# Top-k attention into a mixture of experts on one core: some scores computed ahead and kept in DRAM

## The chip, the core and the metric

One core of a Trainium2 chip runs the whole program. The metric is device time in microseconds (us) of one execution. TensorE (PE) multiplies, VectorE (DVE) searches, ScalarE (ACT) copies and exponentiates, GpSimd (POOL) subtracts and scatters, SyncE (SP) issues most DMAs.

## What is computed

Attention of 8 batches and 8 heads over 576 positions with head size 64, where each row keeps only its 32 largest scores; its output, 4608 rows of 512, goes row by row to the one of 8 experts with the largest gate logit (512 to 1024, ReLU, 1024 to 512).

```python
scores = scale * np.matmul(q, k.transpose(0, 1, 3, 2))
kth = np.partition(scores, -top_k, axis=-1)[..., -top_k:-top_k + 1]
scores = np.where(scores >= kth, scores, -1e9)
attn = softmax(scores)                        # over the last axis
x = np.matmul(attn, v)                        # then (B, S, H*D) -> (4608, 512)
expert_idx = np.argmax(x @ w_gate, axis=1)
# per expert e, for its rows:
y = np.maximum(x_e @ w1[e], 0.0) @ w2[e]
out = gate_w[:, None] * y
```

All of it is float32.

## The kernel before

**Work items.** Two heads make a unit, four units a batch (counted from 0 here and in the code). A row tile is 128 queries of one head; a work item is two row tiles, one of each head of a unit, or the four 64-row tails of two units. So a pair of units has nine items and a batch 18: unit 0's four, a tail item, unit 1's four, and the same again. `loop` (L906) runs over the 144 items in order; one turn is called a slot. Its order is written out by hand for PE, ACT and DVE (`manual_schedule`, L987); SP's and GpSimd's order is left to the scheduler.

**One slot i.** DVE folds the scores of item i+1 (`fold`, L290 and L292; `fold_on`, L298 and L300, late in the slot) and searches the 32nd largest of item i (L329 to L345). ACT turns the threshold into an offset (`low`, L354; `depths`, L370), GpSimd subtracts (`less`, L379), ACT exponentiates (`weights`, L387), PE transposes the weights of item i-1 (`transposed`, L398 to L411) and ACT copies them out (L404, L402, L419). At the end of the slot PE computes the scores of item i+4 (`multiply`, `products`, L276) into two PSUM tiles, which ACT copies into one of four `s` buffers (`scores`, L283) in the next slot. So scores are made with AHEAD = 3 slots in hand. `multiply` also loads the q and k of the unit after next (L141).

**A unit's end.** `ending` is a generator that advances at named places of the slot: attention times v (`outputs`, L432, copied by ACT to oT, L434), its transposition with the gate logits (L443, L450), the divisors (`divisors`: ACT L454 and L455, DVE's reciprocal L457 as one of the small steps in `aside`, of which `tick` puts one behind each search instruction), then GpSimd's `logits` (L465 to L470) and `rows` (L478). After the fourth unit come the choice of the expert, the rank of each row within its expert (`ranks`), and the scatter of the rows to `x_rows` in DRAM (L545).

**Expert blocks.** 128 rows of one expert are a block. `ahead` loads rows and weights of the next blocks on SP (L634, L636, L642; 2 MB each for w1 and w2, two buffers each). `turned` transposes the block's rows (L662, copied by ACT at L664 as xTs); `block` then yields 16 pieces: eight of the first product (L687, four matmuls each) and eight of the second (L702). `pieces(n)` runs up to n of them and stops a block that pauses. Where `current` is None it takes the next loaded block if that was loaded at least ON_CHIP = 3 slots ago. `following`, called within a block, stores results and turns the next block's rows. Each slot deals `now` pieces from a credit: a rate by batch, times a share by the tile, 0.5 to 1.6 (L946). New blocks of a batch reach the list in slot 13 of the next one; a number fixed when the program is built is dealt per batch, and the last 14 blocks and some held back run after the attention, on PE alone.

**PSUM.** `ps_s` has two score tiles; `ps_t` two banks that wTm, wTl, po and px take in turn.

The changed loop's callers are the main body from L734; the code below L1004 runs only where rows stay in doubt.

Of the kernel before, what the change touches and what calls it, by code (L numbers as in the profile page):

```python
# [9 lines left out]
F32 = mybir.dt.float32  # L10
# [25 lines left out]
def kernel(  # L36
# [6 lines left out]
    moe_w2: bass.AP,  # L43
    out: bass.AP,
):

# [34 lines left out]
    nc = tc.nc  # L83
    B, U, P, _ = qk.shape
    N, Dm = out.shape
# [644 lines left out]
    ON_CHIP = 3  # L730
    KEEP = 3 * PIECES
    BETWEEN = 2

    with fast:  # L734
        units = [(b, u) for b in range(B) for u in range(U)]
# [12 lines left out]
        def landed(n):  # L748
            return clock is None or clock - n.at >= ON_CHIP
# [16 lines left out]

        def following():
            put_stores()
            if loaded and landed(loaded[0]):
                turned(loaded[0])  # L770

        def pieces(n):
            nonlocal current, left
            while n > 0 and left > 0:
                if current is None:
                    if not landed(loaded[0]):
                        break
                    current = block(loaded.pop(0), following, stores.append)
                    ahead()
                if clock is None:  # L780
                    evacuate()
                step = next(current)
                if step == "pause":
                    if clock is not None:
                        break
                    continue
                if step == "last":
                    current = None
                n -= 1
                left -= 1  # L790
            return n
# [11 lines left out]
        def ending(b, u):  # L803

            nonlocal left
            n = unit[b * U + u]
            if u == 0:
                x_of[b] = k.xp.tile([P, KC, XW], F32, name="x")
                in_turn(token_ids(x_of[b][:, :, Dm + 1].bitcast(I32), b))
                lg_of[b] = k.small.tile([P, KC, E], F32, name="lg")  # L810
            x, lg = x_of[b], lg_of[b]
            out_steps = outputs(n, x)
            yield "products"
            next(out_steps)
            yield "relu"
            next(out_steps)
            if u % 2 == 0:
                yield "relu"
            div = divisors(n)
            next(div)  # L820
            aside.append(div)
            yield "products"
            next(out_steps)
            if b * U + u + 2 < len(units):
                load_values(unit[b * U + u + 2])
            yield "relu"
            next(out_steps)
            yield "products"
            next(out_steps)
            yield "relu"  # L830
            next(out_steps, None)
            yield "rows"
            through(div)
            logits(n, lg)
            rows(n, x)
            if u < U - 1:
                return
            yield "small"
            r = choice(lg)
            aside.append(r.steps)  # L840
            yield "weights"
            yield "turn"
            through(r.steps)
            nc.scalar.activation(lg, lg, AF.Exp)
            yield "products"
            ranks(r)
            yield "small"
            steps = places(r, x)
            aside.append(steps)
            yield "relu"  # L850
            nc.scalar.copy(run, r.run)
            yield "pool"
            through(steps)
            scatters.extend(scattering(r, x))
            if b == B - 1:
                scatter(KC)
                slot_i = k.small.tile([1, 2, NSLOT], I32, name="slot_i")
                through(table(slot_i, SURE, False))
                firsts = [(slot_i[0:1, 0, j:j + 1], slot_i[0:1, 1, j:j + 1]) for j in range(SURE)]
                ready = load_rows(SimpleNamespace(), firsts[0][1], True)  # L860
            new = LAST - SURE if b == B - 1 else new_of[b]
            if new:
                slot_i = slot_last if b == B - 1 else k.small.tile([1, 2, NSLOT], I32, name="slot_i")
                steps = table(slot_i, new, b == B - 1)
                aside.append(steps)
                yield "weights"
                yield "pool"
                yield "weights"
                yield "pool"
                through(steps)  # L870
                coming.extend((slot_i[0:1, 0, j:j + 1], slot_i[0:1, 1, j:j + 1]) for j in range(new))
            if b == B - 1:
                spare.extend(coming[ALWAYS - SURE:])
                del coming[ALWAYS - SURE:]
                assert len(loaded) == 2 and not waiting
                fill_up()
                coming[0:0] = [(firsts[0][0], ready)] + [(expert, (piece,)) for expert, piece in firsts[1:]]
                scatter(0)
# [9 lines left out]

        got_of, s_of, f_of, w_of = {}, {}, {}, {}

        def tiles_of(i):
            b, g = work[i]
            return [(unit[b * U + u], tile) for u, tile in g]
# [3 lines left out]

        def multiply(i):
            tiles = tiles_of(i)
            got_of[i] = products(tiles)  # L900
            n, tile = tiles[0]
            more = n.b * U + n.u + 2
            if tile == (NC - 1 if n.u % 2 else 2 * NC) and more < len(units):
                unit.append(load_unit(*units[more]))

        def loop():  # L906
            nonlocal credit, rate, clock
            for i in range(min(AHEAD, len(work))):
                multiply(i)
                s_of[i], steps = scores(got_of.pop(i))  # L910
                for step in steps:
                    step()
            multiply(AHEAD)
            f_of[0] = fold(s_of[0])
            fold_on(f_of[0])
            for i, (b, g) in enumerate(work):
                tiles = tiles_of(i)
                u, tile = g[0]
                if tile == 0 and u % 2 == 0:
                    open_unit(tiles[0][0])  # L920
                if tails(tiles):
                    open_unit(tiles[1][0])

                then = lambda: None
                if i + 1 < len(work):
                    f_of[i + 1] = fold(s_of[i + 1])
                    then = lambda: fold_on(f_of[i + 1])
                low, nbias, doubts = search(tiles, s_of[i], f_of.pop(i), then)
                at_place("small")
                w_of[i] = depths(s_of[i], low)  # L930
                less(s_of.pop(i), w_of[i])
                doubts()
                put_stores()
                scatter(1)
                at_place("pool")
                at_place("relu")
                at_place("rows")
                at = i % per_batch
                if at == FIRST and b:
                    rate = new_of[b - 1] * PIECES / (U * NT)  # L940
                credit += rate * len(g)
                room = left
                if b == B - 1 and at >= ARRIVED:
                    room -= KEEP
                    credit = room / (len(work) - i)
                share = {0: 0.5, 1: 1.2, 2: 1.6, 3: 0.5, 2 * NC: 1.4}[tile]  # L946
                now = max(0, min(int(credit * share + 0.5), room))
                credit -= now
                clock = i
                if i + AHEAD < len(work):  # L950
                    s_of[i + AHEAD], steps = scores(got_of.pop(i + AHEAD))
                    for step in steps:
                        step()
                evacuate()
                at_place("turn")
                turns = turning(i - 1) if i else iter(())
                next(turns, None)
                part = min(BETWEEN, now - now // 2)
                rest = pieces(part)
                next(turns, None)  # L960
                rest = pieces(now - now // 2 - part + rest)
                weights(tiles, w_of[i], nbias)
                next(turns, None)
                evacuate()
                if i + AHEAD + 1 < len(work):
                    multiply(i + AHEAD + 1)
                if tile == NC - 1:
                    end = ending(b, u)
                    late.append([end, next(end)])
                at_place("products")  # L970
                at_place("weights")
                credit = min(credit + pieces(now // 2 + rest), 6 * rate)
# [147 lines left out]
```

## Time and profile before

| what | us |
| --- | --- |
| median of ten runs (1371.31 to 1374.38) | 1373.01 |
| the profiled execution | 1372.41 |
| its span | 1370.8 |
| PE busy | 1232.0 (90%) |
| DVE busy | 1084.9 (79%) |
| ACT busy | 931.9 (68%) |
| POOL busy | 661.7 (48%) |
| granted TensorE clock, mean | 0.949 |

A line of the profile's groups reads: line, engine, operation, output from inputs, shape, number of instructions, then total busy time and mean of one in ns, then the idle time in front and what ended it. Timelines give start and length in us. A matmul of float32 appears as two instructions, and their lengths overlap, so the pace of PE is read from starts, not from lengths. DMA rows give size and median time from issue to landing.

### The profile page before, as it was taken

How to read it: one execution, taken by the hardware profiler on the slowest of the kernel's cores; microseconds unless marked ns; L12 is line 12 of the kernel's file. 1: busy time of each engine (PE TensorE's matmuls, PEld its weight loads, DVE VectorE, ACT ScalarE, POOL GpSimd, SP SyncE). 2: the span in 40 equal slices, each digit the busy share in tenths (PEclk: the TensorE clock that was granted, in tenths of full speed). 3: DMA queues.
4: the chain of work that ended last, by engine and by line, in shares of the span. 5: the costliest groups of instructions: out<-in, count | busy, mean ns of one | idle time of the engine just before them, and what ended most of it. 6: DMA issues, size and time to landing. Idle time of an engine off the chain costs nothing. (4 is left out here: it accounts for less than half of the span.)

```text
span 1370.8 us, 24487 instructions
## 1 busy us (share of the span) xinstructions
PE 1232.0 (90%) x7666; PEld 836.5 (61%) x7666; DVE 1084.9 (79%) x4591; ACT 931.9 (68%) x2113; POOL 661.7 (48%) x805
## 2 busy tenths in 40 slices
PE   5777677677799999999999999999999999999995
PEld 3444444344466666766666666767676677776773
DVE  8999999999999999999999999999999820000000
ACT  4788878877888888888877788887777821111110
POOL 3455556555654666566556665565557621000000
PEclk9888887887899999999999999999999999999998
DMA  2000011001573267427654474357542859989880
GB/s 82 29 29 29 28 36 56 29 29 44 182 291 121 92 235 263 141 73 257 231 173 168 162 277 149 113 187 293 184 167 80 303 183 367 383 323 330 302 317 19
DMA packets 102220, 231.68 MB, mean 169 GB/s; under 512 B 5182, under 2 KB 25918, under 8 KB 102080
## 3 DMA queue, kind: packets, MB, share of 16 engines
q1 hardware_dynamic: 95328, 209.76, 43.1%
q0 software_dynamic: 6464, 19.97, 4.0%
q8 instruction: 62, 1.02, 0.3%
q14 instruction: 78, 0.64, 0.1%
q10 hardware_dynamic: 288, 0.30, 0.1%
HBM read 208.72 MB, written 22.33 MB: 169 GB/s over the span
## 5 line engine op out<-in xcount | busy, mean ns | idle before, releaser
L379 POOL TENSOR_TENSOR w<-s,w 128x576 f32<-128x576 f32 x288 | 410.1, 1445 | 432.6 <-ACT w L370 432.6
L687 PE MATMUL ph<-xTs,w 128*128 128x128 f32 x2560 | 308.5, 276 | 6.0 <-ACT xTs L664 6.0
L687 PEld LDWEIGHTS ph<-xTs,w 128*128 128x128 f32 x2560 | 297.5, 192 | 26.2 <-issue 18.9
L702 PE MATMUL py<-w,hT 128*128 128x512 f32 x640 | 292.2, 596 | 0.0
L338 DVE MAX8 tops<-scr 128x8 f32<-128x168 f32 x864 | 245.4, 315 | 0.0
L276 PE MATMUL sc<-qkb 64*128 64x288 f32 (+1 forms) x1280 | 220.6, 470 | 9.5 <-ACT s L283 5.2
L387 ACT ACTIVATE w<-w,nbias 128x576 f32<-128x576 f32 x288 | 224.1, 792 | 2.9 <-POOL w L379 2.0
L370 ACT ACTIVATE w<-s,low 128x576 f32<-128x576 f32 x288 | 207.6, 768 | 4.7
L398 PE MATMUL wTm<-turn,w 128*128 128x128 f32 x1152 | 170.4, 288 | 29.0 <-ACT xl L450 18.9
L999 DVE CAST any_i<-pd 1x1 int32<-1x1 f32 x1 | 0.1, 146 | 236.0 <-PE pd L997 236.0
L398 PEld LDWEIGHTS wTm<-turn,w 128*128 128x128 f32 x1152 | 132.1, 145 | 89.2 <-issue 34.9
L702 PEld LDWEIGHTS py<-w,hT 128*128 128x128 f32 x640 | 114.4, 190 | 117.6 <-issue 116.5
L345 DVE MATCH_REPLACE8 scr<-tops,scr 128x168 f32<-128x168 f32 x576 | 176.9, 311 | 0.0
L283 ACT COPY s<-sc 128x576 f32<-128x576 f32 x288 | 169.1, 641 | 11.0 <-PE sc L276 11.0
L404 ACT COPY wT<-wTm 128x512 f32<-128x512 f32 x256 | 139.1, 604 | 38.9 <-PE wTm L398 38.6
L276 PEld LDWEIGHTS sc<-qkb 64*128 64x128 f32 (+1 forms) x1280 | 117.9, 195 | 72.5 <-issue 26.1
L432 PE MATMUL po<-wT,vb 128*64 128x288 f32 x1024 | 158.6, 459 | 0.4 <-ACT wTt L419 0.4
L708 POOL DMA_INDIRECT out_dram<-y,xg x40 | 43.2, 1079 | 211.7 <-ACT y L716 199.6
L329 DVE MAX8 few<-l 128x8 f32<-128x288 f32 x288 | 127.2, 442 | 0.0
L432 PEld LDWEIGHTS po<-wT,vb 128*64 128x64 f32 x1024 | 75.8, 153 | 79.0 <-issue 31.7
L290 DVE TENSOR_TENSOR h<-s 128x576 f32<-128x576 f32 x144 | 118.4, 822 | 5.8 <-ACT s L283 5.8
L692 ACT ACTIVATE hT<-ph 128x512 f32<-128x512 f32 x80 | 48.6, 608 | 107.3 <-PE ph L687 107.2
(116 smaller groups left out, 1428.8 us busy)
## 6 DMA issues: line engine op xcount, KB each, us to landing
w<-in_moe_w_dram SPq DMA_DIRECT2D x80, 2048.0 KB, 9.6
qkb<-in_qk_dram SPq DMA_DIRECT2D x31, 608.0 KB, 4.0
xg<-x_rows SPq DMA_DIRECT2D x40, 257.0 KB, 9.8
vb<-in_v_dram SPq DMA_DIRECT2D x32, 320.0 KB, 3.2
x_rows<-blank SPq DMA_DIRECT2D x5, 257.0 KB, 13.9
x_rows<-blank POOLq DMA_DIRECT2D x4, 257.0 KB, 8.6
x_rows<-x,posi POOLq DMA_INDIRECT x40, 3.1
out_dram<-y,xg POOLq DMA_INDIRECT x40, 6.1
```

The costliest lines, as they stand in the source:

```text
L276: nc.tensor.matmul(ps[rows, j, 0:HF], n.q[d, cols], n.k[d, keys], start=True, stop=True)
L283: lambda m=m, ps=ps: nc.scalar.copy(s[:, m, :, :], ps[:, :, 0:HF]) for m, ps in enumerate(got)
L338: nc.vector.max(out=tops[:, m, r * 8:(r + 1) * 8], in_=src[m])
L345: nc.vector.match_replace(out=scr[:, m, :], in_to_replace=tops[:, m, r * 8:(r + 1) * 8], in_values=src[m], imm_value=NEG,)
L370: nc.scalar.activation(w[:, m, :], s[:, m, :, :].rearrange("p j k -> p (j k)"), AF.Relu, scale=-STEEP, bias=low[:, m:m + 1],)
L379: k.last_pool = in_turn(nc.gpsimd.tensor_tensor(w[:, m, :], s[:, m, :, :].rearrange("p j k -> p (j k)"), w[:, m, :], op=ALU.subtract)).ins
L387: nc.scalar.activation(w[:, m, :], w[:, m, :], AF.Exp, scale=scale, bias=nbias[:, m:m + 1], accum_out=n.z[:, c:c + 1])
L398: nc.tensor.transpose(pm[:, c * P:(c + 1) * P], w[:, m, first:first + P], ident)
L404: nc.scalar.copy(wT[:, :, m, q], pm4)
L432: nc.tensor.matmul(po[r, 0:HF], n.v[:, c, r], rhs, start=(c == 0), stop=(c == KC - 1))
L687: nc.tensor.matmul(ph[:, f, :], n.w1[:, 0, dt, fc * P:(fc + 1) * P], n.xT[:, dt, :], start=(dt == 0), stop=(dt == DT - 1),)
L702: nc.tensor.matmul(py, hT[:, f, :], n.w2[:, 0, f, :], start=(f == 0), stop=(f == FT - 1))
```

## The change

Four edits.

1. `EARLY_FOR = (4, 5, 6)`. For the four full items of unit 1 in each of these batches (items 5 to 8 of 18), a DRAM tile of 128 x 1152 numbers (576 KB) is set up. A generator `earlier` computes their scores: in each second slot of the first 48 (i odd), between the first transposes and the first pieces, it makes two products of one head into a `sc` tile and copies it on ACT; every second step stores both heads to DRAM on SP. The q and k of a unit (608 KB) sit meanwhile in buffers of the pool `wp`, which otherwise holds w1 and w2. `multiply` leaves these items' products out, and `fetch_scores` loads the stored scores into the `s` buffer on SP in place of ACT's copies.
2. In batches 4 to 6 the share is raised by 0.35 in the slots whose `multiply` has nothing to do, and lowered by 0.1 in the others.
3. A block starts in `pieces` only where its rows have been turned already. `following` turns them if that hasn't been done, and is also called once a slot, behind the weights, where no block is under way.
4. In `ending` the divisors' reciprocal is appended to `aside` one place later, behind the next "relu".

```diff
+    EARLY_FOR = (4, 5, 6)
...
         def following():
             put_stores()
-            if loaded and landed(loaded[0]):
+            if loaded and landed(loaded[0]) and not hasattr(loaded[0], "xT"):
                 turned(loaded[0])
...
                 if current is None:
-                    if not landed(loaded[0]):
+                    if clock is not None and not hasattr(loaded[0], "xT"):
                         break
...
             div = divisors(n)
             next(div)
-            aside.append(div)
             yield "products"
             next(out_steps)
             if b * U + u + 2 < len(units):
                 load_values(unit[b * U + u + 2])
             yield "relu"
             next(out_steps)
+            aside.append(div)
             yield "products"
...
+        early = {}
+        for i, (b, g) in enumerate(work):
+            if b in EARLY_FOR and g[0][0] == 1 and g[0][1] < NC:
+                early[i] = dram.tile([P, 2, 2, HF], F32, name=f"early{i}")
+
+        def earlier():
+            todo = sorted(early)
+            own = []
+            def open_own(p):
+                if p * NC >= len(todo):
+                    return
+                room = k.wp.tile([P, 1, DT, F], F32, name="w1") if p % 2 == 0 else k.wp.tile(
+                    [P, 1, FT, Dm], F32, name="w2")
+                room = room.rearrange("p a b c -> p (a b c)")
+                nc.sync.dma_start(room[:, 0:2 * S + ST], qk[work[todo[p * NC]][0], 1, :, :])
+                own.append(room)
+            open_own(0)
+            for at, i in enumerate(todo):
+                if at % NC == 0:
+                    open_own(at // NC + 1)
+                room = own[at // NC]
+                first = 2 * S + ST + (at % 2) * 2 * S
+                put = room[:, first:first + 2 * S].rearrange("p (m j k) -> p m j k", m=2, j=2)
+                cols = slice((at % NC) * P, (at % NC + 1) * P)
+                for m in range(2):
+                    ps = k.ps_s.tile([P, 2, SM], F32, name="sc")
+                    d = slice(m * D, (m + 1) * D)
+                    for j in range(2):
+                        keys = slice(S + (0 if m else ST) + j * HF, S + (0 if m else ST) + (j + 1) * HF)
+                        nc.tensor.matmul(ps[:, j, 0:HF], room[d, cols], room[d, keys], start=True, stop=True)
+                    nc.scalar.copy(put[:, m, :, :], ps[:, :, 0:HF])
+                    if m:
+                        nc.sync.dma_start(early[i], put)
+                    yield
...
-            got_of[i] = products(tiles)
+            got_of[i] = None if i in early else products(tiles)
...
+        def fetch_scores(i):
+            got = got_of.pop(i)
+            if got is None:
+                s_of[i] = k.att.tile([P, 2, 2, HF], F32, name="s", bufs=4)
+                nc.sync.dma_start(s_of[i], early[i])
+                return
+            s_of[i], steps = scores(got)
+            for step in steps:
+                step()
...
                 share = {0: 0.5, 1: 1.2, 2: 1.6, 3: 0.5, 2 * NC: 1.4}[tile]
+                if b in EARLY_FOR:
+                    share += 0.35 if i + AHEAD + 1 in early else -0.1
...
                 next(turns, None)
+                if i % 2:
+                    next(ahead_of, None)
                 part = min(BETWEEN, now - now // 2)
...
                 weights(tiles, w_of[i], nbias)
                 next(turns, None)
+                if current is None:
+                    following()
                 evacuate()
```

More of the change, by code (lines that the diff above doesn't have):

```diff
@@ L904, in multiply @@
                 unit.append(load_unit(*units[more]))
+        def fetch_scores(i):
[7 more added lines that the diff above has]
+                step()
         def loop():
             nonlocal credit, rate, clock
+            ahead_of = earlier()
             for i in range(min(AHEAD, len(work))):
                 multiply(i)
-                s_of[i], steps = scores(got_of.pop(i))
-                for step in steps:
-                    step()
+                fetch_scores(i)
             multiply(AHEAD)
@@ L950, in loop @@
                 if i + AHEAD < len(work):
-                    s_of[i + AHEAD], steps = scores(got_of.pop(i + AHEAD))
-                    for step in steps:
-                        step()
+                    fetch_scores(i + AHEAD)
                 evacuate()
```

## The prediction

> **What bounds the kernel now.** Batches are counted from 0, as in the code, so the change speaks of batches 4 to 6; a slot is one work item, 18 to a batch. I read the 40 slices first, then a table of windows cut at the batches (by the starts of the fold L290), then the timelines of single slots.
>
> ```profile
> PE   5777677677799999999999999999999999999995
> DVE  8999999999999999999999999999999820000000
> PEclk9888887887899999999999999999999999999998
> ```
>
> Through the attention VectorE shows no idle; from slice 11 TensorE shows none either, and it goes on alone for the last seven slices. Which of the two sets the pace is told by the batches (columns: window, length, busy time of PE, PEld, DVE, ACT, POOL, granted clock):
>
> ```profile
> core 0: us, PE busy (x) PEld busy (x) DVE busy (x) ACT busy (x) POOL busy (x), PEclk, DMA share, GB/s
> 138.50:268.00 129.50, 95.83 (x538) 56.94 (x538) 129.50 (x558) 105.09 (x244) 74.24 (x93) 0.83 0.12 39
> 268.00:398.30 130.30, 101.47 (x602) 64.16 (x603) 130.30 (x573) 104.94 (x243) 73.27 (x92) 0.83 0.35 125
> ...
> 532.40:668.00 135.60, 131.91 (x873) 90.22 (x871) 134.38 (x572) 113.84 (x260) 82.98 (x98) 1.00 0.50 177
> 668.00:813.40 145.40, 144.17 (x963) 100.78 (x962) 142.02 (x573) 115.54 (x265) 87.14 (x99) 1.00 0.56 198
> 813.40:949.00 135.60, 131.90 (x872) 90.23 (x871) 134.38 (x573) 113.82 (x260) 82.98 (x98) 1.00 0.50 178
> ```
>
> The same 573 VectorE instructions take 130.3 us in batch 2, where TensorE is idle for 28.8 us, and 135.6, 145.4, 135.6 us in batches 4, 5, 6, where it is idle for 3.7, 1.2, 3.7. So 130.3 us is VectorE's floor, and the 5.3, 15.1 and 5.3 us above it come from TensorE. In batch 1 TensorE has 33.7 us to spare and ScalarE 24.4. Batch 7 and the tail are TensorE's again, so what TensorE gains in batches 4 to 6 reaches the end unless it is given back as new idle.
>
> **The change, part by part.**
>
> *Products taken out of batches 4 to 6.* Twelve items (four of each batch) lose their score products and two ScalarE copies. One item's products, L276, run from their own start to that of the next group:
>
> ```profile
> 663.38 1.24 PE L276 MATMUL sc<-qkb 64*128 64x288 f32 x8
> 664.55 0.64 PE L443 MATMUL px<-turn,oT 128*128 128x144 f32 x3
> ```
>
> That is 1.17 us, so 4.7 a batch and 14.0 in all. The copies, 24 of 641 ns, are 15.4 us of ScalarE, which is not the bound; I count nothing for them.
>
> *Pieces dealt anew.* By the built order of instructions batches 4, 5 and 6 hold 68, 76 and 68 block pieces before and after; none leaves for the tail. The largest lump grows: slot 1 of batch 5 gets 13 pieces (before 9), slot 2 none (before 4). Over both the sum is equal: 0 us.
>
> *What is given back.* TensorE can't run ahead of what the slot's search releases:
>
> ```profile
> 610.00 0.66 PE L398 MATMUL wTm<-turn,w 128*128 128x128 f32 x4
> 611.70 0.66 PE L398 MATMUL wTm<-turn,w 128*128 128x128 f32 x4 [1.05 <-ACT oT L434]
> ```
>
> Here, in slot 9 of batch 4, it already waits 1.05 us for a bank that ScalarE empties only behind that slot's search. By then it is 4 x 1.17 = 4.7 us lighter, but VectorE can come forward only by its own stalls: slots 4 and 7 took 9.41 and 9.11 us between starts of L290, 7.66 and 7.89 in batch 2, so 1.75 + 1.22 = 3.0. The other 1.7 us turn into idle: 3.4 us for batches 4 and 6. Batch 5 has 15.1 us of room and keeps its 4.7. Bounds: 0 (the stalls at the batch's end shrink too), and 2 x 4.7 = 9.4.
>
> *Early scores.* 24 steps, in each second slot of the first 48, each two products of one head and a copy of 0.64 us. The trace shows no such step: at least half an item, 0.6 us of TensorE; at most four instructions of 0.40 us side by side in time, 1.6 us, and 1.9 at the clock of 0.83. I take 1.2. Cover: TensorE's 33.7 us and ScalarE's 24.4 us idle in batch 1, 1.9 and 1.4 a slot. What pays is not the sum but the lateness: each copy stands ahead of the slot's two exponentials, so ScalarE, and behind it the subtraction on GpSimd (L379), end later, and GpSimd meets VectorE's folds. What that costs is in the trace:
>
> ```profile
> 202.83 1.48 POOL L478 TENSOR_TENSOR x<-xl,rz 128x640 f32<-128x640 f32 x1
> 203.58 1.33 DVE L290 TENSOR_TENSOR h<-s 128x576 f32<-128x576 f32 x1
> ```
>
> The fold, 0.73 us elsewhere, waits until L478 ends: 0.6 us. I take such a stall in 3 or 4 of 24 steps, +2 us; bounds 0 and 24 x 0.6 = 14.4, nearer to 0 because ScalarE's spare time of two slots, 2.7 us, exceeds copy and wait (0.64 + 1.2).
>
> The Trainium skill (TensorE: Matmul & The Clock Gate, Part 3, The mechanism) speaks against this step: small products overlap when they sit in different row groups, and the step takes one head, so one row group. The trace agrees that pairs overlap, since eight instructions of 0.40 us fit into 1.24. By the rule an early item costs double, 2.3 us, or 28 in all; were early TensorE the bound, that would turn the sum to the slow side, but its rows there are idle for 33.7 us a batch.
>
> *Stores and fetches.* Three loads of 608 KB and twelve stores of 576 KB fall into slices with DMA at 0 to 2 tenths: nothing. They stand on SP's queue among the loads of qk and v; each of those is issued some four slots ahead of its use. The twelve fetches wait on SP until GpSimd has left a score buffer, about 5 us into slot i, and are needed at the start of slot i+2: 2 x 7.2 - 5 = 9.4 us. The nearest rows:
>
> ```profile
> w<-in_moe_w_dram SPq DMA_DIRECT2D x80, 2048.0 KB, 9.6
> qkb<-in_qk_dram SPq DMA_DIRECT2D x31, 608.0 KB, 4.0
> ```
>
> Alone a fetch has 5.4 us to spare. The built order puts six of them right behind a weights load, where qk landed after 7.9 us (579.01 to 586.89): 1.5 us to spare, less wherever ScalarE lags. Queued behind them on SP are weights that are needed a block later. I take +1 us; bounds 0 (and a gain of the DVE waits for L283, 5.8 us in all) and 6 x 1.0 = 6.
>
> *First blocks' rows ahead.* Five batches (3 to 7) under TensorE's bound begin their first block with a wait:
>
> ```profile
> PE ph L687 <- ACT xTs L664: 6.0, 6, 1.1
> ```
>
> Now the rows are turned behind wTl (L411), then come 1.17 us of products, then the block. But the copy L664 moves behind both exponentials (2 x 0.79 + 2 x 0.21 = 2.0 us) and wTt's 0.27: with y's copy (0.58) and its own 0.5 xTs is ready 3.3 us behind wT's copies, and TensorE gets there in 0.16 + 0.44 + 1.17 = 1.8. Wait 1.5 instead of 1.2: +0.3 each, +1.5. Bounds: -6.0 (all gone) and +2.8.
>
> *Reciprocals.* Queued for VectorE a slot later. DVE rz waited 2.5 us each in batches 5 and 7, where TensorE sets the pace: 0, at best -2.5.
>
> **Sum**: -14.0 + 3.4 + 2 + 1 + 1.5 = -6.1. The profiled execution took 1372.4 us (span 1370.8, 1.6 around it), the median of the ten is 1373.0; from the first 1366.3, from the median 1366.9.
>
> **Rivals.**
> *More arrives*: the xTs waits vanish (-6.0 in place of +1.5): 1366.9 - 7.5 = 1359.4. For it: 1.17 us of cover is the wait's own size. Against: the copy's new place.
> *Nothing arrives*: the fetches are late and VectorE becomes the bound of batches 4 and 6. Three fetches there that stand 3.1 us too long behind weights, within the 3.9 us that these cost qk (7.9 against 4.0), eat the two batches' 9.4 us: 1373.0 - 14.0 + 9.4 + 2 + 1 + 1.5 = 1372.9. For: a margin of 1.5 us, and at SP one waiting weights load holds all behind it (L634 waited 75.8 us for L687). Against: TensorE's backlog takes up a short VectorE stall.
> *Slower*: the early steps. All 24 make GpSimd collide with a fold: 1373.0 - 14.0 + 3.4 + 14.4 + 1 + 1.5 = 1379.3; it decides from 8.1 / 24 = 0.34 us a step. VectorE has no idle there, so every stall counts in full. Against: ScalarE's 1.4 us spare a slot.
> That the change does nothing is out: the built order shows the twelve items' products gone, 48 early ones added.
>
> **How the numbers follow.** A measurement here tells 0.2% (2.7 us) from no change. Forecast 1361 to 1370: 0.52, all faster. More arrives: 0.10. Nothing arrives: 0.17, of which 0.14 within 0.2% and 0.03 slower. Slower: 0.21, of which 0.02 within. Faster 0.62, same 0.16, slower 0.22. The range, 1359 to 1376, holds the forecast, half of the better case, nearly all of the third and 0.07 of the slow one.
>
> **What will show it.** Batches 4, 5, 6 at about 132.6, 140.7, 132.6 us, with more PE waits on oT (L438 in the new lines). Batches 0 to 2 at 127.7, 129.5, 130.3 us plus at most 2 in all; more there is the slow rival. DVE waits on the DMA s<-early would be late fetches, PE waits on xTs above 1.2 us the moved rows. I am wrong if batches 4 and 6 don't shorten though early slots cost nothing: then TensorE was not their bound.

## The result and the profile after

The changed kernel takes 1378.95 us (median of eight, 1375.88 to 1379.51) against 1372.96 for the kernel before, timed beside it: ratio 1.0040, 95% interval 1.0031 to 1.0048. It is slower by 5.5 us where 6.1 us less was forecast. Its profiled execution took 1378.43 us, span 1376.8, 6.0 more than before. A second set of runs of the same kernel gave 1378.38 us, ratio 1.0037 (1.0022 to 1.0051).

The slices of the changed kernel's page answer to the three rows shown of before:

```profile
PE   6888888787899999999999999999999999999995
DVE  8999999999999999999999999999999820000000
PEclk9797889887899999999999999999999999999998
```

TensorE is a little busier in ten of the first eleven slices, VectorE as full as before. The windows, cut at the changed kernel's own batches (1, 2, 4, 5, 6; columns as before):

```profile
core 0: us, PE busy (x) PEld busy (x) DVE busy (x) ACT busy (x) POOL busy (x), PEclk, DMA share, GB/s
139.00:270.10 131.10, 107.80 (x580) 64.95 (x579) 131.10 (x558) 109.51 (x254) 77.21 (x95) 0.86 0.17 57
270.10:405.30 135.20, 114.76 (x642) 72.06 (x642) 135.20 (x572) 110.38 (x253) 74.95 (x93) 0.87 0.39 138
538.00:673.40 135.40, 128.47 (x841) 88.42 (x840) 135.40 (x573) 109.41 (x252) 83.52 (x98) 0.99 0.55 195
673.40:819.30 145.90, 142.27 (x933) 100.06 (x932) 142.08 (x571) 112.67 (x258) 84.29 (x99) 0.99 0.60 213
819.30:954.10 134.80, 127.05 (x838) 86.85 (x837) 134.80 (x573) 108.55 (x251) 83.18 (x98) 1.00 0.56 196
```

Batches 4, 5 and 6 last 135.4, 145.9 and 134.8 us (135.6, 145.3, 135.6 before), although TensorE now is idle for 6.9, 3.6 and 7.8 us of them in place of 3.7, 1.2 and 3.7. TensorE's busy time in the three fell by 10.2 us and its idle time rose by 9.7: the work was taken off it and became idle time. Batches 1 and 2 grew by 1.6 and 4.9 us, without any idle time of VectorE: the same instructions took longer.

The waits of the changed kernel over the whole program (engine, line, what ended the wait: sum, times, longest):

```profile
PE ph L691 <- ACT xTs L668: 6.5, 6, 1.3
PE wTm L402 <- ACT oT L438: 6.2, 9, 1.2
...
DVE pos L528 <- ACT run L856: 4.7, 2, 2.9
...
PE wTm L402 <- DVE pos L528: 4.1, 2, 2.0
```

Before, TensorE waited 3.5 us for oT (4 times) and not for `pos`, the rank of a row within its expert. The wait for xTs, 6.0 before, is 6.5. In batches 4 to 6 alone (window 532:955) the changed kernel has the 4.1 us for `pos` and

```profile
PE wTm L402 <- ACT oT L438: 2.3, 4, 1.1
PE wTm L402 <- ACT xl L454: 2.0, 2, 1.0
```

where the kernel before has 2.1 us for oT and none for `xl` or `pos`. So the new idle of these batches is not the wait for oT that the prediction named; that one grew with the old dealing only (`core` and `no_share`, below).

Where the six microseconds are, from the starts of the fold of each batch's first item:

| us | before | changed | difference |
| --- | --- | --- | --- |
| batches 0 to 2 | 387.4 | 394.4 | +7.0 |
| batch 3 | 134.1 | 132.7 | -1.4 |
| batches 4 to 6 | 416.6 | 416.1 | -0.5 |
| batch 7 | 130.2 | 130.4 | +0.2 |
| from there to the end of the span | 291.6 | 292.3 | +0.7 |

So two things are to be explained: why the early steps cost several microseconds, and why 14 us of TensorE's work brought half a microsecond.

### The profile page after: what moved, and what is told of

Same layout as the page of the kernel before. It is cut to its first block, busy times and chain, and to the rows that moved or that the text cites. A ratio compares the mean times of both kernels' runs of the same rounds, so it can differ in the third digit from the quotient of the medians.

```text
span 1376.8 us, 24546 instructions
## 1 busy us (share of the span) xinstructions
PE 1260.2 (92%) x7666; PEld 853.7 (62%) x7666; DVE 1094.8 (80%) x4591; ACT 931.2 (68%) x2113; POOL 661.8 (48%) x805
## 5 line engine op out<-in xcount | busy, mean ns | idle before, releaser
L383 POOL TENSOR_TENSOR w<-s,w 128x576 f32<-128x576 f32 x288 | 410.1, 1445 | 438.5 <-ACT w L374 438.4
L280 PE MATMUL sc<-qkb 64*128 64x288 f32 (+1 forms) x1184 | 216.1, 472 | 9.6 <-ACT s L287 5.2
L287 ACT COPY s<-sc 128x576 f32<-128x576 f32 x264 | 154.8, 640 | 9.9 <-PE sc L280 9.9
L408 ACT COPY wT<-wTm 128x512 f32<-128x512 f32 x256 | 138.9, 601 | 32.9 <-PE wTm L402 32.4
L294 DVE TENSOR_TENSOR h<-s 128x576 f32<-128x576 f32 x144 | 114.8, 797 | 4.0 <-ACT s L287 3.1
```

The source lines that it names most:

```text
L280: nc.tensor.matmul(ps[rows, j, 0:HF], n.q[d, cols], n.k[d, keys], start=True, stop=True)
L287: lambda m=m, ps=ps: nc.scalar.copy(s[:, m, :, :], ps[:, :, 0:HF]) for m, ps in enumerate(got)
L383: k.last_pool = in_turn(nc.gpsimd.tensor_tensor(w[:, m, :], s[:, m, :, :].rearrange("p j k -> p (j k)"), w[:, m, :], op=ALU.subtract)).ins
L408: nc.scalar.copy(wT[:, :, m, q], pm4)
```

## What an early step costs: one slot of batch 2

Slot 7 of batch 2 took 7.89 us before and 10.26 in the changed kernel. The timeline of that slot before (start, length, engine, line, operation; parts of it):

```profile
319.00 0.21 ACT L354 ACTIVATE low<-tops 128x2 f32<-128x2 f32 x1 [0.15 <-DVE tops L338]
320.10 2.84 POOL L379 TENSOR_TENSOR w<-s,w 128x576 f32<-128x576 f32 x2 [4.44 <-ACT w L370]
322.79 0.17 DVE L589 CAST ci<-run 1x8 int32<-1x8 f32 x1
323.13 0.18 DVE L591 TENSOR_SCALAR ci<-ci 1x8 int32<-1x8 int32 x1
```

And in the changed kernel:

```profile
319.44 2.28 PE L928 MATMUL sc<-w 64*128 64x288 f32 x4
...
321.76 0.64 ACT L929 COPY w<-sc 128x576 f32<-128x576 f32 x1 [1.63 <-PE sc L928]
...
324.50 0.20 ACT L358 ACTIVATE low<-tops 128x2 f32<-128x2 f32 x1
...
325.59 2.78 POOL L383 TENSOR_TENSOR w<-s,w 128x576 f32<-128x576 f32 x2 [7.00 <-ACT w L374]
325.66 1.37 DVE L593 CAST ci<-run 1x8 int32<-1x8 f32 x1
...
327.19 1.20 DVE L595 TENSOR_SCALAR ci<-ci 1x8 int32<-1x8 int32 x1
```

ScalarE waits 1.63 us for the early product and copies it, and only then come the two exponentials and `low`: 2.7 us into the slot, 0.1 before. So GpSimd's two subtractions (L383) start at 325.59, in the very moment at which VectorE handles the eight counters `ci`. A cast of eight numbers takes 1.37 us in place of 0.17 and ends when the first subtraction ends; the next takes 1.20 in place of 0.18 and ends with the second. VectorE is "busy" all that time. The same slot in seven kernels shows a dose and its effect:

| kernel | `low` starts in the slot at | the slot lasts |
| --- | --- | --- |
| before | 0.11 us | 7.89 us |
| placed (below) | 0.11 | 7.89 |
| placed_early_only (below) | 0.57 | 8.30 |
| early_only (below) | 1.73 | 9.11 |
| core (below) | 1.79 | 9.18 |
| changed, second set | 2.32 | 9.82 |
| changed | 2.74 | 10.26 |

The other seven kernels below fall into the same order: 0.12 and 0.17 us go with 7.89 and 7.88, three times 0.55 or 0.56 with 8.28 or 8.29, 1.13 with 8.94 and 2.00 with 9.52. Where the reciprocals are moved, 0.19 us of the slot is one of them.

All of batches 0 to 2 can be accounted for in this way. Take what each VectorE instruction needs above the lower quartile of its form (same operation, tiles and shape) in the kernel before, leave out differences under 0.1 us, and add up: call this the excess. It is 3.6 us before and 10.6 in the changed kernel, and the 7.0 between them are the whole growth. Each of the ten instructions that lose at least 0.5 us (two before) starts while a GpSimd instruction runs and ends no sooner than that one.

## The experiments

Each kernel was timed beside the kernel before. "Batches" are lengths in its profiled execution.

### Early steps alone (early_only)

Against the changed kernel: dealing, first rows and reciprocals as before, and the stored scores aren't used; batches 4 to 6 compute their own.

```diff
-            got_of[i] = None if i in early else products(tiles)
+            got_of[i] = products(tiles)
```

> The early products, copies and stores alone; the stored scores are not used, the 12 items keep their own products, and the dealing, the first blocks' rows and the reciprocals are as before. Theory A (the early steps stall VectorE in batches 0 to 2, and nothing came back later): batches 0 to 2 lengthen by about 7 us in all, as in the changed kernel (128.1, 131.1, 135.2 us), batches 3 to 7 stay, the time is about 1380. Theory B (the loss of batches 0 to 2 comes from the moved reciprocals or rows): batches 0 to 2 as before within 1 us, the time 1373 to 1375.

1377.08 us, ratio 1.0025 (1.0015 to 1.0035): +3.4 us. Batches 0 to 2 392.7 (+5.3), batch 3 132.3 (-1.8), batches 4 to 6 unchanged at 416.6. The early steps cost 3.4 us by themselves; the moved reciprocals and rows aren't needed for that. The loss is where the first theory put it, and smaller than its 7 us. Of the 5.3 us, 1.1 are VectorE's waits for the divisors (`rz`), which the changed kernel, with its moved reciprocals, doesn't have there.

### First blocks' rows alone (first_only)

Of the change only the turning of first rows ahead: no early scores, reciprocals as before.

```diff
-    EARLY_FOR = (4, 5, 6)
+    EARLY_FOR = ()
```

> Only the first blocks' rows turned ahead; no early scores, dealing and reciprocals as before. Theory A: between -1.5 and +1.5 us. Theory C (the copy of the turned rows, now behind both exponentials, delays ScalarE and so GpSimd and the folds): +3 us or more, with the folds L302 and L304 lengthened in slots 15 to 17.

1375.50 us, ratio 1.0010 (1.0001 to 1.0020): +1.4 us. Batch 3 grows by 0.4 and batches 4 to 6 by 0.9 together; TensorE's wait for xTs rises from 6.0 to 7.1 us. The price agrees with the 1.5 us foretold; its interval is 0.1 to 2.7.

### The change without the rows ahead (no_first)

```diff
-                if current is None:
-                    following()
```

with the two conditions on `xT` back to `landed`.

> The changed kernel with the first blocks' rows turned as before. Theory A: 1379, within 1.5 us of the changed kernel. Theory C: 1375 or less, with slots 15 to 17 of batches 4 to 6 shorter by 1 us.

1374.66 us, ratio 1.0009 (0.9999 to 1.0018). Without them the changed kernel is 4 us faster by the ratios, more than the rows cost alone. Batches 4 to 6 take 415.4 us, 0.7 less than in the changed kernel; the rest of the difference lies in batches 0 to 3, 524.0 against 527.1. That is one execution each, and such stretches scatter: the next kernel has the same instructions as the changed one there, and took 525.3. Of the 3.1 us, 2.5 lie before slot 14 of batch 2, up to where the two kernels have the same instructions in the same order on every engine, so they can't come from the rows. Nor does the sign of the theory that came nearer in time show: slots 15 to 17, which were to be 1 us shorter, are 0.3 us shorter in batches 4 and 6 and no shorter in batch 5.

### The change with pieces dealt as before (no_share)

```diff
-                if b in EARLY_FOR:
-                    share += 0.35 if i + AHEAD + 1 in early else -0.1
```

> The changed kernel with the pieces dealt as before. Theory A (TensorE's relief turns into its own idle because VectorE and GpSimd bound batches 4 and 6): 1379, batches 4 to 6 together 416 us as in the changed kernel. Theory D (the new dealing eats the gain, by the 13 pieces of slot 1 of batch 5 and by fuller late slots): batches 4 to 6 together 408 to 411 us, the time 1371 to 1374.

1373.43 us, ratio 0.9999 (0.9988 to 1.0009). Batches 4 to 6 take 411.0 us against 416.1: the dealing, put down at 0 in the prediction, costs 5.1 us there and some 5.6 by the ratios. That is what the second theory foretold (408 to 411 us, 1371 to 1374).

### The changed kernel again (after_again)

> The changed kernel once more, so that it stands beside the parts on one chip: 1.004 of the kernel before, as before, if nothing but chance lies between the calls; nearer to 1.002 if its first rounds were drawn high.

1378.38 us, ratio 1.0037. Batches 0 to 3 take 527.4 us and batches 4 to 6 415.6, close to the first profile.

### Early scores alone (core)

The first of the four edits alone: dealing, rows and reciprocals as before.

> Only the early scores: computed, stored and fetched, with dealing, first blocks' rows and reciprocals as before. Theory A (the late part keeps some 5.5 us of its 14.0 because TensorE turns the rest into waits for ScalarE's oT, for the rank bank and for a late fetch, and the early part costs 3 to 5): batches 4 to 6 together 411 us (416.5 before, 416.1 changed), batches 0 to 2 together 391 to 394, the time 0.997 to 1.000 of the kernel before. Theory D' (rows and reciprocals matter too): 1.001 or more.

1372.64 us, ratio 0.9999 (0.9986 to 1.0011): no change. Batches 0 to 3 525.3 (+3.8), batches 4 to 6 411.7 (-4.9). The idea of the change, by itself, returns what it costs. In batch 5, which was to keep 4.7 us, 0.7 is left: 145.3 to 144.6.

### Early steps in another place (placed)

Against `core`: a step takes one half of both heads, whose products run side by side, into two banks of the blocks' first product; it stands behind the slot's exponentials, so ScalarE copies it when `low` is not waiting.

```diff
-                for m in range(2):
-                    ps = k.ps_s.tile([P, 2, SM], F32, name="sc")
-                    d = slice(m * D, (m + 1) * D)
-                    for j in range(2):
+                for j in range(2):
+                    both = [k.ps_m.tile([P, SM], F32, name="ea", tag="m") for m in range(2)]
+                    for m, ps in enumerate(both):
+                        d = slice(m * D, (m + 1) * D)
...
-                if i % 2:
-                    next(ahead_of, None)
                 part = min(BETWEEN, now - now // 2)
...
                 weights(tiles, w_of[i], nbias)
                 next(turns, None)
+                if i % 2:
+                    next(ahead_of, None)
```

> As the last, but an early step makes both heads' products of one half side by side, into the block's two PSUM banks (free until the first block), behind the weights' exponentials and ahead of the slot's own products, instead of between the transposes. Theory A (the early cost is ScalarE's lateness: the copy ahead of the exponentials and the wait for its products): batches 0 to 2 come back to 389 us or less (387.5 before), the time to 0.994 to 0.997. Rival E (the cost comes from the work itself, or from loads and stores on SP): batches 0 to 2 stay at 391 to 394 us.

1371.12 us, ratio 0.9983 (0.9973 to 0.9992): faster than both kernels. Batches 0 to 2 390.2 in place of 393.0, between theory A (389 or less, with a ratio of 0.994 to 0.997) and rival E (391 to 394). Batch 3 gives 1.9 us back (132.4 to 134.3). Slot 7 of batch 2 is back at 7.89 us; in four later kernels with this place it took 8.28 to 8.30. One step occupies TensorE for 0.69 us (median, from its start to the next group's), against 1.17 for one head. Batch 5 took 143.0, with one long wait of VectorE, in its slot 4. The timeline there (start, length; SPq are DMAs issued by SP):

```profile
691.70 0.39 SPq L638 DMA_DIRECT2D w<-in_moe_w_dram  x1
692.21 7.66 SPq L955 DMA_DIRECT2D s<-early  x2
...
704.53 0.76 DVE L294 TENSOR_TENSOR h<-s 128x576 f32<-128x576 f32 x1 [3.34 <-DMA s<-early]
```

A load of 2 MB of weights was issued at 691.70, and the fetch at 692.21. The fetch's median is 4.3 us to land; this one, the slowest of the twelve, took 12.2.

### Fetches issued by ScalarE (placed_actq)

```diff
-                nc.sync.dma_start(s_of[i], early[i])
+                nc.scalar.dma_start(s_of[i], early[i])
```

> As the last, with the twelve fetches issued by ScalarE instead of SP, so that no weights load stands ahead of them in a queue. Theory A: batch 5 loses its DVE wait of 1.8 us for the fetch, batches 4 to 6 together 409 us; the time 1 to 2 us below the last. Rival: issuing on ScalarE costs it as much as the copies did, nothing or a loss.

1369.93 us, ratio 0.9977 (0.9967 to 0.9986). No fetch took more than 7.6 us to land, but in ScalarE's order the fetch of batch 5's first item went out at 699.20, 7.8 us after its buffer was free (691.41); VectorE waited 3.6 us in all and batch 5 took 143.2. One delay had replaced the other, and the time isn't told apart from that of `placed`.

### Fetches issued by ScalarE ahead of the offset (placed_ahead)

```diff
+                if i + AHEAD in early:
+                    fetch_scores(i + AHEAD)
                 low, nbias, doubts = search(tiles, s_of[i], f_of.pop(i), then)
```

> Early steps in the better place; the stored scores are fetched by ScalarE in front of the slot's first offset (about 7.0 us into the slot, 2.6 us behind the buffer's release), neither on SP behind a weights load of 2 MB nor, as in the run before, about 10.3 us into the slot. Theory A (in batch 5 a fetch that lands late eats what TensorE gained): VectorE's waits for s<-early below 1 us in all, against 3.3 and 3.6; batch 5 at 140 to 141 us, against 143.0 and 143.2; time about 1367. Rival B (without the late fetch VectorE waits for oT or the rank's bank instead): batch 5 at about 143, time about 1370 to 1371.

1370.99 us, ratio 0.9975 (0.9966 to 0.9984); batch 5 144.3; the time isn't told apart from that of the last two. My theory missed: the waits for s<-early fell only to 2.0 us (one fetch still took 9.2 us to land), and batch 5 became no shorter. The rival is nearer. In the waits of batches 4 to 6 of this kernel TensorE's wait for oT is the largest of its data waits:

```profile
PE wTm L402 <- ACT oT L438: 7.3, 5, 2.5
```

against 2.1 us in the kernel before. Slots 3 and 4 of batch 5, where the fetches were late, became hardly shorter: together 18.1 us before, 18.9 in `core`, 18.9 in `placed` and 18.6 here. VectorE's instructions tell why. In `placed` the wait for the fetch is 3.3 us, and one small operation (L494) loses 0.6 us behind a subtraction of GpSimd. Here the wait is 1.7 us, but two of them (L494 and L496) take 1.16 and 1.14 us in place of 0.18, each until a subtraction ends. What the earlier fetch gave, collisions took. In `placed_share` (below) the two slots have neither and take 14.7.

### The better place alone (placed_early_only)

`placed`, with the stored scores unused as in `early_only`.

> Only the early steps, in their better place (both heads' products of one half side by side, in two banks of the blocks' first product, behind the exponentials); the scores that they store are fetched by nobody, batches 4 to 6 compute all their own. Theory A (an early step costs by the lateness that it gives to ScalarE and GpSimd, and this place costs less than the change's, which took 5.2 us in batches 0 to 2): batches 0 to 2 at about 390.2 us in place of 387.5, batches 4 to 6 as before at about 416.5, time about 1375.5. Rival B (the late place is free, and what batches 0 to 2 lost there is scatter): 387.5 in batches 0 to 2, time about 1373.

1376.98 us, ratio 1.0021 (1.0012 to 1.0030): +2.9 us, batches 0 to 2 389.8, batches 4 to 6 416.6. The rival (free) falls; but the better place saves less time than the profile's 2.9 us in batches 0 to 2 says (392.7 to 389.8), since batch 3 gives 2.0 back (132.3 to 134.3). Against `early_only` it isn't told apart by time alone.

### The new dealing on the better place (placed_share)

`placed` and the two lines of the new dealing.

> The kernel with early steps in the better place, and the change's new dealing of pieces on top, nothing else of the change. Theory A (the new dealing itself makes VectorE wait in batches 4 to 6): batches 4 to 6 at about 415 to 416 us, against 410.1 with the old dealing, time about 1375 to 1377. Rival B (the dealing cost only together with the moved rows of the first blocks): batches 4 to 6 at about 410, time about 1371.

1373.93 us, ratio 0.9999 (0.9991 to 1.0008), against 0.9983 for `placed`: some 2 us by the ratios, 5.2 by batches 4 to 6 (415.3 against 410.1). The length is what the theory that the dealing itself makes VectorE wait foretold, the time lies between the two theories. Slot 4 of batch 4 shows how: 8.48 us in `placed`, 10.05 here, and the same in batch 6. In `placed`:

```profile
564.14 1.25 POOL L482 TENSOR_TENSOR x<-xl,rz 128x640 f32<-128x640 f32 x1
...
566.26 3.05 POOL L383 TENSOR_TENSOR w<-s,w 128x576 f32<-128x576 f32 x2 [0.18 <-ACT w L374]
...
569.51 0.18 DVE L494 TENSOR_TENSOR oh<-lg,mx 128x40 f32<-128x40 f32 x1
...
569.91 0.18 DVE L496 TENSOR_TENSOR oh<-oh,e_less 128x40 f32<-128x40 f32 x1
```

With the new dealing:

```profile
567.06 1.26 POOL L482 TENSOR_TENSOR x<-xl,rz 128x640 f32<-128x640 f32 x1
568.46 2.76 POOL L383 TENSOR_TENSOR w<-s,w 128x576 f32<-128x576 f32 x2
568.73 0.17 DVE L492 TENSOR_REDUCE mx<-lg 128x5 f32<-128x40 f32 x1
569.06 0.86 DVE L494 TENSOR_TENSOR oh<-lg,mx 128x40 f32<-128x40 f32 x1
570.15 1.13 DVE L496 TENSOR_TENSOR oh<-oh,e_less 128x40 f32<-128x40 f32 x1
```

Slot 2 holds more pieces there, ScalarE's copy of px (L454) came at 562.02 in place of 560.17, and so GpSimd did the unit's rows (L482) 2.9 us later and the slot's subtractions 2.2 us later, on top of VectorE's choice of the expert: 0.86 and 1.13 us for two instructions of 0.18, which is 1.63 us, all that the slot grew by (1.57). In batch 5 two slots pay: slot 5 takes 8.1 us in place of 7.0 and slot 6 10.5 in place of 7.6, and there `pos` waits 1.8 us for ScalarE's `run`; slots 3 and 4, without the late fetch, give 4.2 us back.

### Two units of batch 5 (placed_five)

As `placed_ahead`, 24 early steps again, but for units 1 and 3 of batch 5 and unit 1 of batch 6, none of batch 4.

```diff
-    EARLY_FOR = (4, 5, 6)
+    EARLY_FOR = ((5, 1), (5, 3), (6, 1))
...
-            if b in EARLY_FOR and g[0][0] == 1 and g[0][1] < NC:
+            if (b, g[0][0]) in EARLY_FOR and g[0][1] < NC:
...
-                nc.sync.dma_start(room[:, 0:2 * S + ST], qk[work[todo[p * NC]][0], 1, :, :])
+                nc.sync.dma_start(room[:, 0:2 * S + ST], qk[work[todo[p * NC]][0], work[todo[p * NC]][1][0][0], :, :])
```

> As the run with the fetch in front of the offset, with the same 24 early steps for other units: two units of batch 5 (units 1 and 3) and one of batch 6, none of batch 4. Theory A (only batch 5 has room between TensorE and VectorE's floor of 130.3 us; batches 4 and 6 have it for half a unit): batch 4 back at about 135.5, batch 5 at 136 to 137, batch 6 at 133.5; time about 1364 to 1366. Rival B (VectorE's own waits end the gain in batch 5 after one unit): batch 5 at 140 to 143, time 1369 to 1372.

1367.81 us, ratio 0.9957 (0.9943 to 0.9970), the best of all: 5.9 us faster than before. Its windows of batches 4, 5 and 6:

```profile
534.70:670.30 135.60, 131.92 (x873) 90.34 (x872) 134.38 (x572) 113.82 (x260) 82.89 (x98) 1.00 0.50 178
670.30:809.20 138.90, 134.79 (x902) 95.84 (x901) 135.82 (x572) 108.10 (x251) 82.89 (x101) 1.00 0.66 233
809.20:942.40 133.20, 126.15 (x836) 86.95 (x835) 132.09 (x573) 108.96 (x251) 80.26 (x96) 1.00 0.59 206
```

Batch 4 is back at 135.6, batch 5 gained 6.4 us, of the 9.4 us of work taken out there. The same steps bring more in the batch that was furthest above VectorE's 130.3 us. But 138.9 and 1367.8 us lie between the two theories, not in the first.

## Why the prediction was wrong

| step | foretold | measured | from |
| --- | --- | --- | --- |
| products out of 4 to 6, what is given back, fetches | -14.0 + 3.4 + 1 = -9.6 | -4.9, -5.6 | batches 4 to 6 in `core`, `no_share` |
| pieces dealt anew | 0 | +5.1 | batches 4 to 6, changed less `no_share` |
| early steps | +2 | +3.4 | ratio of `early_only` |
| first blocks' rows | +1.5 | +1.4 | ratio of `first_only` |
| sum | -6.1 | +4.3 to +5.0; the whole change +5.5 | |

The first two rows are lengths in single profiles and the next two are ratios of times, so the sum is rough: by the ratios (`core` against `early_only`) the first row is -3.6.

**The failed step is "Over both the sum is equal: 0 us"**, the dealing. I counted pieces over two slots and asked whether TensorE has the same work. The work is the same, and slots 1 and 2 of batch 5 together last 14.4 us in `no_share` and in the changed kernel. But its order decides when px and the ranks are ready, and so when GpSimd is in VectorE's way. The price is paid elsewhere: slots 5 and 6 of batch 5 went from 14.6 to 19.8 us (3 and 4 gave 3.5 back), slot 3 of batches 4 and 6 from 7.1 to 8.4 and 8.9. With the old dealing the change is at 0.9999.

**The second is the size of what is given back.** In batches 4 and 6 the forecast was 3.0 us kept of 4.7; `core` and `no_share` kept 2.1 and 2.2, with the waits for oT that the prediction named (7.7 and 6.1 us in batches 4 to 6, 2.1 before). In batch 5 "keeps its 4.7" was wrong: 0.7 and 1.1 were kept. Behind it lies a misreading of the table of windows. I put the 15.1 us above 130.3 down to TensorE as a whole, so that less work had to shorten it one for one. But VectorE was busy for 142.0 of the 145.4 us, and for 134.4 of the 135.6: most of the 15.1 us isn't idle time, it is VectorE's own instructions taking longer, in the slots followed above behind GpSimd's. Counting VectorE instructions in batches 4 to 6 that take at least 0.5 us more than the lower quartile of their form in the kernel before, there are 23 before, 22 in the changed kernel, 20 in `placed_share`, 19 in `no_share`, 16 in `core`, 15 in `placed` and 14 in `placed_five`. Each of them starts while a GpSimd instruction runs and ends no sooner than it. The changed kernel had lightened TensorE and kept these stalls. The excess as defined above and VectorE's idle time account for batches 4 to 6 (us):

| kernel | length | excess | VectorE idle | rest |
| --- | --- | --- | --- | --- |
| before | 416.6 | 22.4 | 5.8 | 388.4 |
| changed | 416.1 | 24.1 | 3.8 | 388.2 |
| `placed_share` | 415.3 | 21.0 | 5.8 | 388.5 |
| `core` | 411.7 | 16.1 | 7.5 | 388.1 |
| `no_share` | 411.0 | 18.7 | 4.5 | 387.8 |
| `placed` | 410.1 | 14.0 | 8.0 | 388.1 |
| `placed_five` | 407.7 | 14.2 | 5.4 | 388.1 |

The rest is the same in all, 129.4 us a batch: VectorE undisturbed. Of the 25.7 us that the prediction put down to TensorE, VectorE was idle in at most 5.8. With the new dealing the excess grows by 5.4 us (`no_share` to changed) and by 7.0 (`placed` to `placed_share`).

**The early steps** were of the foretold size on TensorE (1.17 us each, 1.2 foretold), and the mechanism was the one named, GpSimd meeting VectorE: the term is mis-sized, +3.4 in place of +2. Its premise, that only the folds are hit, at 0.6 us each, was too narrow: the two counters' instructions of one slot lost 2.2 us by themselves. The slow rival named the right mechanism and almost the right time (1379.3), but by 24 stalls, 14.4 us, where the steps cost 3.4. That its time came close is luck: the dealing (+5.1) and the products' smaller return (-4.9 in place of -9.6) brought the rest.

**Right** were the price of the rows (though the waits that it starts from, put at 1.2 us each, are six of 1.0 on average in the line shown), and that a fetch could be late behind a weights load. It was late in `placed`, `core` and `no_share`. In the changed kernel one wait of 0.9 us was left: the fetch of batch 5's third early item was issued at 717.53, as soon as its buffer was free, 3.8 us ahead of its fold.

**Open** is what the rows cost in company. By the ratios the changed kernel is 4 us faster without them, and alone they cost 1.4; with the old dealing they cost nothing that shows (0.9999 with them and the moved reciprocals in `no_share`, 0.9999 without in `core`). Taken as they are, the ratios say that rows and dealing cost more together than apart. The profiles don't show where: of the 4.2 us between the spans of the changed kernel and `no_first`, 2.5 lie where both have the same instructions. The four executions with these instructions (changed, its second set, `no_share`, `no_first`) took 365.2, 365.0, 363.4 and 362.7 us from the start of batch 0 to slot 14 of batch 2, and why they differ isn't known. The reciprocals weren't tried by themselves.

## What to carry to other kernels

An engine that shows as busy can be blocked: compare the time of the same instructions in a stretch with and without company before putting the extra time down to a slower engine next to it. Work taken off an engine is worth something only where what it releases comes earlier, so look at what each wait is ended by, and reckon with a new order of the same work costing as much as the work was worth. Take relief to the stage that is furthest above its floor: the same 24 early steps were worth 3.4 us in three batches and 5.9 with two thirds of them in the one that was furthest behind.

## What the hardware showed

That a GpSimd instruction blocks VectorE's two-input folds was known from the kernel before. Not expected was that it blocks instructions with one input too, and the smallest: a cast of eight numbers took 1.37 us in place of 0.17 and a scalar operation on eight 1.20 in place of 0.18, each ending with a subtraction of GpSimd. In `placed_share` a reduction (L492) that ran within a subtraction kept its 0.17 us, while two operations on 40 numbers took 0.86 and 1.13.

The Trainium skill (SBUF — State Buffer, Who interferes with whom) states that VectorE and GpSimd share a pair of ports that one instruction holds to its end, and that casts and scalar operations can take it, reductions not. The runs agree in all three, with the numbers above.

A transfer of 576 KB that was issued 0.5 us behind one of 2 MB took 12.2 us to land in `placed`, 11.6 in `core` and 10.1 in `no_share`; the medians of its kind in these kernels were 4.3 to 4.7.
